# Two w_gate transfers of a GeGLU kernel on ScalarE's DMA queue: one issued three copies later, one taken over from SP's queue

## The chip, the cores and the metric

The kernel runs on one core of a Trainium2 chip. The metric is the device time of one execution in microseconds (us). Three runs of the kernel before took 275.5, 275.68 and 275.7 us; the median is 275.68 us.

## The reference

x is a bf16 tensor of 32 x 32 x 1024 values, seen as a 1024 x 1024 matrix (1024 tokens, D = 1024). w_gate and w_up are 1024 x 3584 (F = 3584), w_down is 3584 x 1024, all bf16.

```python
def reference(x, w_gate, w_up, w_down):
    return (_gelu(x @ w_gate) * (x @ w_up)) @ w_down     # _gelu: the tanh approximation
```

## The kernel before

Two stages follow each other: gate and up products with the Gelu between them (lines 131 to 353), then the product with w_down (lines 355 to 512). Each uses a scheme that needs seven block products in place of eight (sums of blocks are formed on VectorE, GpSimd and ScalarE first, then multiplied). The change touches only the start of the first stage.

The first stage works with transposed data: F is on the partitions, 28 blocks of 128 columns of F, and the tokens are the moving dimension, in two halves of 512. D is split in two halves of four 128-row pieces each (KH = 4). So there are four blocks of x: B11 and B21 (first 512 tokens, first and second half of D, together the tile xt0) and B12 and B22 (the other tokens, the tile xt1). The weights are a11 and a12 (the two halves of w_gate's rows for one block of F), a21 and a22 (those of w_up).

The order of the work is written out by hand (`tc.manual_schedule()`), and each engine and each DMA queue takes its own instructions in program order. What matters around the change:

- **Transposes of x**, all on SP's queue: L131 loads B11, L149 loads B21, L154 loads xt1. The one of L149 waits for a small ScalarE instruction (L147) that ends at 5.65 us.
- **w_gate** comes in tiles of two blocks of F, WG[c] for blocks 2c and 2c+1, each with a first half (`0, KH`, for a11) and a second half (`KH, DT`, for a12). `load_gate(c, queue, lo, hi)` (L83, the transfer in L86) loads a part of one: a half is 256 KB. WG[4] and WG[5] lie in parts of gT, the result of the stage, that are written much later; the others in a ring of four buffers.
- **ScalarE's queue** carries at the start (L140 to L145) the first halves of WG[0] to WG[3] and the second half of WG[0], and at L280 the second half of WG[1].
- **SP's queue** carries, behind the transpose of B21 (L149 to L157): the second half of WG[2], half of the first w_up tile WU[0], the second half of WG[3], all of WG[4], the transpose of xt1, the two halves of WG[5], the other half of WU[0]; later WG[6] (L319), which waits for a free buffer.
- **`first_products(n)`** (L204): four matmuls of block n, a11 by B11, then a ScalarE copy of the product (L212). **`second_products(n)`** (L214): four matmuls a12 by B21 onto the same PSUM bank, then a ScalarE Gelu (L219).
- PE's order is `first_products` of 0 and 1 together and of 2 to 7 one by one (L279 to L282), `second_products` of 0 to 7 (L283), `first_products` of 8 and 9, `second_products` of 8 and 9, `first_products(10)` (LEAD, L292), and then the products with sums of x: fifth (Y, with T1, L298), sixth (X, with T2), seventh (T3), fourth (T4). So block 2 is the first to use WG[1] in both parts, block 8 the first to use WG[4], block 10 the first to use WG[5].
- **The sums of x**: VectorE forms T1 to T4 (L166, called in L275 to L278) from xt1 and xt0; T1 in four pieces, the others in two each.

Of the kernel before, what the change touches and what calls it, by code (L numbers as in the profile page):

```python
# [12 lines left out]
def kernel(  # L13
# [18 lines left out]
    nc = tc.nc  # L32
# [10 lines left out]
    DT = D // P  # L43
    KH = DT // 2
# [38 lines left out]
    def load_gate(c, queue, lo=0, hi=DT):  # L83
        if c not in WG:
            WG[c] = gw.tile([P, DT, 2 * P], bf16, name="gw", tag="gw")
        queue.dma_start(  # L86
            out=WG[c][:, lo:hi, :], in_=wg_r[:, lo:hi, 2 * c * P : (2 * c + 2) * P]
        )
# [12 lines left out]
    def a11(i):  # L101
        return block(WG, 2, i, 0)

    def a12(i):
        return block(WG, 2, i, 1)
# [18 lines left out]
    def psum_p(name):  # L124
        return psum.tile([P, NB], fp32, name=name, tag="p")

    def psum_q(name):
        return psum.tile([P, NB], fp32, name=name, tag="q")

    with tc.manual_schedule():  # L130
# [21 lines left out]
        load_gate(3, nc.sync, KH, DT)  # L152
        load_gate(4, nc.sync)
        nc.sync.dma_start_transpose(out=xt1, in_=xf[NB:N, :])  # L154
        load_gate(5, nc.sync, 0, KH)
        load_gate(5, nc.sync, KH, DT)
        load_up(0, 2, 4)  # L157

# [32 lines left out]
        def pair_product(ps, lhs, rhs, first, cuts):  # L191
            for lo, hi in zip(cuts, cuts[1:]):
                for p, l in zip(ps, lhs):
                    for k in range(lo, hi):
                        nc.tensor.matmul(  # L195
                            p,
                            lhsT=l[:, k, :],
                            rhs=rhs[:, k, :],
                            start=(first and k == 0),
                            stop=(k == KH - 1),  # L200
                            skip_group_check=True,
                        )

        def first_products(*blocks, cuts=(0, KH)):  # L204
            for i in blocks:
                A[i] = psum_p("a") if 4 <= i < 8 else psum_q("a")
            pair_product([A[i] for i in blocks], [a11(i) for i in blocks], B11, True, cuts)
            for i in blocks:
                if i % 2 == 0:
                    pool, tag = (xpool, "e1") if i == LEAD - 2 else (ring, "ring")  # L210
                    E1[i // 2] = pool.tile([P, 2, NB], fp32, name="e1", tag=tag)
                nc.scalar.activation(E1[i // 2][:, i % 2, :], A[i], ACT.Copy)  # L212

        def second_products(*blocks, cuts=(0, KH)):  # L214
            pair_product([A[i] for i in blocks], [a12(i) for i in blocks], B21, False, cuts)
            for i in blocks:
                if i % 2 == 0:
                    GL[i // 2] = half.tile([P, 2, NB], bf16, name="gl0", tag="half")
                nc.scalar.activation(GL[i // 2][:, i % 2, :], A[i], ACT.Gelu_apprx_tanh)  # L219
# [3 lines left out]
        def seed(i):  # L223
            X[i] = psum_p("x")
            nc.scalar.activation(X[i], E1[i // 2][:, i % 2, :], ACT.Copy)
# [51 lines left out]
        t_sum("T3", B22, B12)  # L277
        t_sum("T4", B21, T["T2"])  # L278
        first_products(0, 1, cuts=(0, 2, KH))  # L279
        load_gate(1, nc.scalar, KH, DT)  # L280
        for n in range(2, 8):
            first_products(n)  # L282
        for n in range(8):  # L283
            second_products(n)
            if n in (5, 6):
                seed(n - 5)
        first_products(8)
# [255 lines left out]
```

## Time and profile before

| | |
|---|---|
| median of the runs | 275.68 us |
| the profiled execution | 275.76 us |
| its span, first to last instruction | 273.9 us |
| granted TensorE clock | 1.000 |
| PE (TensorE matmul) busy | 268.7 us, 98% of the span |
| VectorE, ScalarE, GpSimd busy | 69%, 51%, 32% |
| DMA in the whole span | 26.42 MB, mean 96 GB/s |
| DMA from 5.67 to 26.5 us | 269 to 311 GB/s |

How to read the lines that the prediction quotes: times are in us from the start of the span. A line of the timeline has the start, the duration, the engine, the source line, the operation, the tiles out<-in, shapes, the number of instructions merged in the line, and in brackets the idle time before it with what ended it. PE is TensorE's matmuls, PEld its weight loads, DVE is VectorE, ACT is ScalarE, POOL is GpSimd. SPq and ACTq are the DMA issues of SP and of ScalarE: their duration is that of the issue, not of the transfer; the time from issue to landing stands in another view. A line of the chain of waits has start, duration and what the chain ran through. A line of the table by stretches has the stretch, its length, the busy time and number of instructions of PE, PEld, DVE, ACT and POOL, the granted clock, the DMA share and GB/s.

### The profile page before, as it was taken

The numbers are of one execution on the slowest core, as the hardware profiler recorded it, in microseconds if no ns is written. First come the engines' busy times: TensorE is split into PE (matmuls) and PEld (weight loads), VectorE is DVE, ScalarE is ACT, GpSimd is POOL, SyncE is SP. The second block draws the span as 40 slices with busy tenths as digits, with TensorE's granted clock in tenths as the row PEclk, the third lists the DMA queues.
The fourth block names the chain that finished last, engine by engine and source line by source line (L and its number), as shares of the span: only waits on it lengthen the run. The fifth ranks groups of instructions, "written<-read, shape, count | busy, mean of one in ns | idle before, by whom it ended". The sixth has DMA issues, their size and how long they took to land.

```text
span 273.9 us, 3338 instructions
## 1 busy us (share of the span) xinstructions
PE 268.7 (98%) x1172; PEld 189.4 (69%) x1186; DVE 189.2 (69%) x226; ACT 139.7 (51%) x240; POOL 87.2 (32%) x81
## 2 busy tenths in 40 slices
PE   8999999999999999999999999999999999999995
PEld 2445677778777787776877768764447888888883
DVE  0078885866658666586665866769994999999900
ACT  4778665566565665666655666531100072860311
POOL 0000075745557455584555845600000000000000
PEclk9999999999999999999999999999999999999999
DMA  7999402153300034216360202369602000000321
GB/s 185 277 288 247 154 1 77 52 180 110 121 2 0 0 103 130 77 35 196 96 213 0 77 5 74 107 190 334 214 0 77 2 0 1 0 2 0 116 77 38
DMA packets 41024, 26.42 MB, mean 96 GB/s; under 512 B 9264, under 2 KB 41008, under 8 KB 41008
## 3 DMA queue, kind: packets, MB, share of 16 engines
q1 hardware_dynamic: 37680, 24.51, 30.5%
q10 hardware_dynamic: 3328, 1.70, 2.3%
q8 instruction: 9, 0.15, 0.2%
q14 instruction: 7, 0.06, 0.1%
HBM read 22.02 MB, written 2.10 MB: 88 GB/s over the span
## 4 chain that ended last, share of the span: by engine, by line
PE 94%; DMA 4%; ACT 1%; issue 0%
PE x L195 19%; PE x L398 18%; PE y L115 18%; PE a L195 15%; PE y L398 9%; PE x L115 9%; PE z L398 4%; DMA xt<-in_x_dram 3%; DMA gw<-in_w_gate_dram 1%; PE y L195 1%; ACT L139 0%; ACT o_sb L510 0%
## 5 line engine op out<-in xcount | busy, mean ns | idle before, releaser
L195 PE MATMUL x<-T,s 128*128 128x512 f32 x224 | 63.4, 407 | 0.0
L195 PEld LDWEIGHTS x<-T,s 128*128 128x128 f32 x224 | 41.7, 188 | 10.9 <-ACT e L242 0.3
L195 PE MATMUL a<-xt,gw 128*128 128x512 bf16 x182 | 44.1, 380 | 1.1 <-DMA xt<-in_x_dram 0.3
L259 DVE TENSOR_TENSOR u<-y,e 128x512 bf16<-128x512 f32 x28 | 19.3, 691 | 31.8 <-ACT e L257 30.9
L184 POOL TENSOR_TENSOR s<-gw,s 128x512 fp32r<-128x512 bf16 x22 | 26.0, 1182 | 47.6 <-PE y L115 46.9
L180 DVE TENSOR_TENSOR s<-s,gw 128x512 fp32r<-128x512 f32 x24 | 34.9, 1456 | 0.0
L195 PEld LDWEIGHTS <-gw 128*128 128x128 bf16 x192 | 17.1, 98 | 24.8 <-issue 5.2
L266 ACT ACTIVATE gl<-h 128x512 bf16<-128x512 bf16 x28 | 17.7, 631 | 27.5 <-DVE h L264 27.5
L246 DVE TENSOR_TENSOR gT<-gl,x 128x512 bf16<-128x512 bf16 x28 | 19.2, 686 | 17.9 <-PE x L115 17.9
L115 PE MATMUL x<-T,c 128*128 128x512 f32 x112 | 30.3, 392 | 0.0
L115 PE MATMUL y<-B,s 128*128 128x512 f32 x112 | 30.2, 391 | 0.0
L175 POOL TENSOR_TENSOR s<-uw 128x512 fp32r<-128x512 bf16 x25 | 29.1, 1165 | 0.0
L115 PE MATMUL y<-T,s 128*128 128x512 f32 x104 | 27.8, 389 | 0.0
L398 PE MATMUL x<-tc,sc 128*128 128x512 f32 x112 | 25.7, 389 | 0.0
L257 ACT ACTIVATE e<-x 128x512 f32<-128x512 f32 x28 | 16.7, 600 | 16.0 <-PE x L195 16.0
L176 POOL TENSOR_TENSOR s<-gw,uw 128x512 fp32r<-128x512 bf16 x21 | 24.5, 1167 | 0.0
L115 PEld LDWEIGHTS y<-B,s 128*128 128x128 f32 x112 | 21.0, 188 | 4.8
L212 ACT ACTIVATE e<-a 128x512 f32<-128x512 f32 x28 | 16.6, 597 | 15.2 <-PE a L195 15.2
L115 PEld LDWEIGHTS x<-T,c 128*128 128x128 f32 x112 | 20.9, 188 | 4.8 <-ACT e L257 0.4
L398 PEld LDWEIGHTS x<-tc,sc 128*128 128x128 f32 x112 | 21.0, 188 | 4.4
L115 PEld LDWEIGHTS y<-T,s 128*128 128x128 f32 x104 | 19.5, 188 | 4.1
L219 ACT ACTIVATE gl<-a 128x512 bf16<-128x512 f32 x28 | 16.7, 597 | 7.1 <-PE a L195 7.0
(58 smaller groups left out, 342.0 us busy)
## 6 DMA issues: line engine op xcount, KB each, us to landing
uw<-in_w_up_dram SPq DMA_DIRECT2D x6, 1024.0 KB, 6.4
gw<-in_w_gate_dram SPq DMA_DIRECT2D x8, 512.0 KB, 4.0
v<-in_w_down_dram SPq DMA_DIRECT2D x5, 512.0 KB, 3.8
v<-in_w_down_dram SPq DMA_DIRECT2D x4, 640.0 KB, 8.1
v<-in_w_down_dram SPq DMA_DIRECT2D x8, 256.0 KB, 4.2
out_dram<-o_sb SPq DMA_DIRECT2D x15, 128.0 KB, 1.7
gw<-in_w_gate_dram ACTq DMA_DIRECT2D x5, 256.0 KB, 5.0
uw<-in_w_up_dram SPq DMA_DIRECT2D x2, 512.0 KB, 5.4
```

Source lines behind the costliest of these rows:

```text
L115: nc.tensor.matmul(ps, lhsT=lhs[:, k, :], rhs=rhs[:, k, :], start=(first and k == 0), stop=(k == KH - 1), skip_group_check=True,)
L175: engine.tensor_tensor(S1[i], a21(i), a22(i), ALU.add)
L176: engine.tensor_tensor(S3[i], a11(i), a21(i), ALU.subtract)
L180: nc.vector.tensor_tensor(S2[i], S1[i], a11(i), ALU.subtract)
L184: engine.tensor_tensor(S4[i], a12(i), S2[i], ALU.subtract)
L195: nc.tensor.matmul(p, lhsT=l[:, k, :], rhs=rhs[:, k, :], start=(first and k == 0), stop=(k == KH - 1), skip_group_check=True,)
L219: nc.scalar.activation(GL[i // 2][:, i % 2, :], A[i], ACT.Gelu_apprx_tanh)
L246: nc.vector.tensor_tensor(gT[:, i, 0:NB], GL[i // 2][:, i % 2, :], X[i], ALU.mult)
L257: nc.scalar.activation(e3, X[i], ACT.Copy)
L259: nc.vector.tensor_tensor(U1[i], Y[i], e3, ALU.add)
L266: nc.scalar.activation(G1[i], h1, ACT.Gelu_apprx_tanh)
L398: nc.tensor.matmul(ps, lhsT=lhs[:, i, t * P : (t + 1) * P], rhs=rhs[:, i, :], start=(first and j == 0 and i == 0), stop=(last and j == JF ...
```

## The change

The second half of WG[1] is still loaded over ScalarE's queue, but its issue stands behind the copy of `first_products(3)` (the fourth copy) and no longer behind the first two. The first half of WG[5] is no longer issued by SP, behind the transpose of xt1, but by ScalarE, behind the Gelu of `second_products(1)` (the second Gelu). Its second half stays on SP's queue. No instruction is added or removed.

```diff
         nc.sync.dma_start_transpose(out=xt1, in_=xf[NB:N, :])
-        load_gate(5, nc.sync, 0, KH)
         load_gate(5, nc.sync, KH, DT)
         load_up(0, 2, 4)
...
         first_products(0, 1, cuts=(0, 2, KH))
-        load_gate(1, nc.scalar, KH, DT)
         for n in range(2, 8):
             first_products(n)
+            if n == 3:
+                load_gate(1, nc.scalar, KH, DT)
         for n in range(8):
             second_products(n)
+            if n == 1:
+                load_gate(5, nc.scalar, 0, KH)
             if n in (5, 6):
                 seed(n - 5)
```

## The prediction

> **What bounds the kernel now.** I read the page first. Its first part says that TensorE is what the span consists of, and the chain of work that ended last says the same (PE 94%, DMA 4%):
>
> ```profile
> PE 268.7 (98%) x1172; PEld 189.4 (69%) x1186; DVE 189.2 (69%) x226; ACT 139.7 (51%) x240; POOL 87.2 (32%) x81
> ```
>
> So the change can win only where the chain is not PE. I then took the chain in order of time over the first 36 us. It leaves PE in two places: the first weights (until 5.41) and one transpose of x:
>
> ```profile
> 5.41 0.26 PE a L195
> 5.67 7.18 DMA xt<-in_x_dram
> 12.86 0.14 issue
> 12.99 1.67 PE a L195 x7
> ```
>
> The transpose is that of L149 (B21): issued at 5.67, landed at 12.86, and `second_products(0)` starts at 12.99. What the wait costs is not the 0.28 us that the waits list shows for it (matmuls overlap). I read it from ScalarE, which copies one product each time PE has done four matmuls:
>
> ```profile
> 10.16 0.60 ACT L212 ACTIVATE e<-a 128x512 f32<-128x512 f32 x1 [0.27 <-PE a L195]
> 11.02 0.60 ACT L212 ACTIVATE e<-a 128x512 f32<-128x512 f32 x1 [0.27 <-PE a L195]
> 11.89 0.60 ACT L212 ACTIVATE e<-a 128x512 f32<-128x512 f32 x1 [0.27 <-PE a L195]
> 12.75 0.60 ACT L212 ACTIVATE e<-a 128x512 f32<-128x512 f32 x1 [0.27 <-PE a L195]
> 14.05 0.60 ACT L219 ACTIVATE gl<-a 128x512 bf16<-128x512 f32 x1 [0.70 <-PE a L195]
> ```
>
> The step is 0.863 us (0.216 per matmul). After the copy at 12.75 the next event is due at 13.61 and comes at 14.05: PE lost **0.44 us**, and from 13 us on PE has no further stall before 24 us. 0.44 us is 0.16% of the time. Less than 0.2% (0.55 us) is about what a measurement of this kernel cannot tell from no change.
>
> Last, why does the transpose land so late? The timelines of SP's queue and of ScalarE's:
>
> ```profile
> 5.67 3.97 SPq L149 DMA_TRANSPOSE xt<-in_x_dram  x1
> 7.54 0.37 ACTq L86 DMA_DIRECT2D gw<-in_w_gate_dram  x1
> 9.70 0.58 SPq L86 DMA_DIRECT2D gw<-in_w_gate_dram  x1
> 12.46 6.84 SPq L154 DMA_TRANSPOSE xt<-in_x_dram  x1
> 19.34 1.13 SPq L86 DMA_DIRECT2D gT<-in_w_gate_dram  x2
> 21.52 2.50 DVE L166 TENSOR_TENSOR T<-xt,xt 128x512 fp32r<-128x512 bf16 x4 [1.04 <-DMA xt<-in_x_dram]
> ```
>
> The ACTq row at 7.54 is the second half of WG[1] (I call it the gate-1 tail), issued in the middle of the transpose's issue. The first row at 19.34 holds two issues: WG[5]'s first half (the gate-5 head) and its second. The trace also holds a record of each DMA packet. There the transpose's data packets run from 8.6, when ScalarE's earlier transfers run out, to 11.05. Then the gate-1 tail's 256 KB run on the same engines from 11.0 to 11.85, and only at 11.77 to 11.86 come the transpose's 32 four-byte packets, which end it. For the two other transposes these packets come with the last data (data to 4.35, packets at 4.20 to 4.39; data to 20.9, packets at 20.91 to 20.95). So the gate-1 tail stands between the transpose's data and its landing for 0.7 us. The moved rate has a hole before that, too:
>
> ```profile
> 8.00:9.00 1.00, 1.00 (x6) 0.49 (x5) 0.00 (x0) 0.75 (x2) 0.00 (x0) 1.00 1.21 284
> 9.00:10.00 1.00, 1.00 (x7) 0.43 (x5) 0.00 (x0) 0.63 (x2) 0.00 (x0) 1.00 1.34 168
> 10.00:11.00 1.00, 1.00 (x6) 0.45 (x5) 0.00 (x0) 0.60 (x1) 0.00 (x0) 1.00 1.27 289
> ```
>
> The last column is GB/s: in 9 to 10 some 120 KB were not moved, about 0.42 us at 289. Whether the 7.54 issue made that hole the trace does not show.
>
> **Part 1, the gate-1 tail behind the fourth copy.** ScalarE issues a DMA when it has sent off the copy before it, not when the copy ends: the 7.54 issue stands between the first copy's start (7.10) and the second's (7.60). So the new issue comes with the fourth copy, at 9.30: 1.76 us later. Cost on ScalarE: 0.37 us (the row above) against 0.26 us idle per step; the next copy is 0.11 us late, and the step after has it back. The first user of a freed PSUM bank, `first_products(8)`, comes at 19.89, 5 us behind the first Gelu's end. So this costs nothing; without that cover it would be 0.37.
>
> Gain: if the transpose ends with its data, its end packets come at 11.1 in place of 11.8, and it lands at about 12.15 or earlier (12.86 - 0.7). PE's next weight load is due at 12.34 (last at 12.12, step 0.216), and it began 0.10 behind the landing: a landing by 12.24 loses nothing. So the whole 0.44 returns. The bounds: 0 (the order of the packets stays), and 0.44, for then PE's own work ends last, whatever else the queue gains.
>
> What is late next: the gate-1 tail itself. `second_products(2)` loads its weights at 14.50 now, at 14.06 with PE 0.44 earlier. On an idle queue the first packet came 1.04 us after the issue (28.64, 40.80); so its data can run from 11.05, 256 KB at 289 GB/s take 0.91, and it lands between 12.5 and 13.0. Cover 1 us. SP's next, the second half of WG[2], shares that stretch, lands at 13.50 now, and is needed at 16.2: cover 2.7 us, 2.2 after the shift.
>
> **Part 2, the gate-5 head on ScalarE's queue.** SP's row at 19.34 loses one issue (0.58 us), so the WG[5] tail and the last half of WU[0] follow at once, 0.6 earlier; WG[6] waits at 21.08 for its buffer, as now. ScalarE issues at the second Gelu, 14.91 now, 14.47 shifted: 0.37 to 0.57 us (five issues in 2.83 at the start) beside 0.26 idle per Gelu, so up to 0.3 us late, made good in two Gelus, and nobody waits until 19.89.
>
> What it removes is a limit that part 1 would run into. The gate-5 head lands now at 19.34 + 3.7 = 23.04, and `first_products(10)` loads its first weights at 23.14: 0.10 us of cover. With PE 0.44 earlier alone, 0.34 would be lost there. Issued at 14.5 it is there by 22.4 even if it is served only behind the whole third transpose (data to 20.9, then 0.91, then 0.6 to land). Cover 0.3 of the shifted need at 22.70.
>
> What it adds: 256 KB ahead of the landing of the third transpose (12.46 + 9.0 = 21.46), on which DVE's T1 waits (1.04 us idle). At 289 GB/s that is **0.91 us**. The bounds: 0 (served later), and 1.7, if it meets all that the second transpose meets now (0.91 of data, the hole's 0.42, and some 0.3 of increments behind the other's). I take 0.91: the transfer has the size of the gate-1 tail, whose packets took 0.85. Cover: T1's fourth piece ends at 24.02 and the matmul that reads it starts at 25.60; T2's second half ends at 26.29, its reader starts at 27.86. Both leave 1.57, less 0.07 from DVE to PE: 1.50, and 1.06 with PE shifted. 0.91 fits, by 0.15. T3, T4 have 2.0.
>
> **Sum**: -0.44 (part 1) + 0 (ScalarE) + 0 (part 2 uses up cover only) = -0.44. The profiled execution took 275.76 us (span 273.9 and 1.86 around it): 275.32. The median of the runs is 275.68, 0.08 lower: 275.24. I say **275.3**.
>
> **The rivals.**
>
> *The landing stays (A).* The new issue at 9.30 still falls before SP has finished issuing the transpose (9.64). If what counts is that ScalarE's transfer comes into the queue before the transpose's end packets do, the order stays, B21 lands at 12.86, and part 2 has its 1.5 us of cover: 275.7. For it: with 1.04 from issue to data the tail is ready at 10.34, before the data end at 11.05. Against: so was the first transfer of ScalarE (issue 1.83) while the first transpose ran until 4.35, and that one's end packets were not held up. The Trainium skill (DMA: Bandwidth & Descriptors, section "Queues, rings and completion order") says that the increment of a semaphore lands only after every earlier write of that DMA engine, across its queues. By that rule B21 lands late as long as the tail's data is taken first, which is this rival; the end packets at 11.77 agree with it.
>
> *ScalarE's queue is left waiting (B), the slower side.* The second transpose was issued at 5.67 and had no packet until 8.6, exactly as ScalarE's backlog ran dry. If a queue with work keeps the engines, the reverse holds: the gate-1 tail, now issued only 0.4 us ahead of SP's 9.70, waits behind WG[2]'s half and WU[0] and lands where that lands now, at 15.33, against a need at 14.06. From a landing after 14.0 it costs PE time: 15.4 + 0.1 - 14.06 = 1.4, less the 0.44: 276.7 and more if the gate-5 head, needed at 22.70, meets the same. Against: at 11.0 the tail got in although SP's transfer of 9.70 should have been ready at 10.74. The same section of the Trainium skill says that an engine goes round the queues that have work, packet by packet; by that rule this rival falls. The trace shows no such mixing around 8.6, so I keep the rival.
>
> *The third transpose is later than 0.91 (C).* At 1.2 to 1.7, T1 and T2 exceed their 1.06 by 0.15 to 0.65: 275.4 to 275.9.
>
> *A stall that I do not see goes too (D)*: below 275.1.
>
> **How the numbers follow.** Forecast 0.52, A 0.17, B 0.13, C 0.12, D 0.06. Faster by over 0.2% (below 275.13) takes D and 0.06 of the forecast, which ends 0.1 to 0.2 us from that line: 0.12. Slower by over 0.2% (above 276.23) takes B and 0.03 of C: 0.16. Within: 0.72. The range runs from 275.0 to 276.7: it takes in A, C and B's price for the gate-1 tail alone, and leaves out B's worse end and most of D.
>
> **What would show it.** Right: no chain piece of the L149 transpose behind PE's last `first_products` matmul; its landing by 12.3; the first Gelu at 13.6; the first product on gT at 19.45; T1 beginning by 22.5 with PE unbroken from 24 to 28. Part 1 wrong: the first Gelu still at 14.05 (A), or a PE wait on gw near 14.1 (B). Part 2 wrong: a PE wait on gT near 22.7, or on DVE T between 23.6 and 28 (C).

## The result, and the profile after

The changed kernel takes 276.0 us (median of 22 runs, 275.55 to 276.88) against 275.68 us for the kernel before (22 runs beside them, 275.02 to 276.2). The ratio is 1.0013, with a 95% interval of 1.0008 to 1.0019: slower by a little more than a tenth of a per cent, where 275.3 us, 0.14% faster, had been forecast. All ratios here leave out an execution more than 1.5% above the fastest of its kernel; there was one such, of 279.78 us, in after_third below. The profiled execution of the changed kernel took 275.71 us (span 273.9). That is near the low end of its runs; a profile of a longer one comes below.

I read the new profile in the order of the old one. The busy times of the page are the same within 0.1 us on every engine: nothing has changed in the amount of work. Then ScalarE's timeline of the changed kernel around the first Gelu, with start, duration, engine, line and idle time (the lines of the kernel file have moved up by one behind the edit):

```profile
12.69 0.60 ACT L211 ACTIVATE e<-a 128x512 f32<-128x512 f32 x1 [0.27 <-PE a L194]
13.55 0.60 ACT L218 ACTIVATE gl<-a 128x512 bf16<-128x512 f32 x1 [0.27 <-PE a L194]
14.42 0.40 ACTq L86 DMA_DIRECT2D gT<-in_w_gate_dram  x1
```

The step of 0.863 us now runs on from the last copy (12.69) to the first Gelu (13.55). The 0.44 us that PE lost there are gone. The last copy was 0.06 us earlier already (12.69 against 12.75), so the first Gelu is 0.50 us earlier than before (14.05). Part 1 did what it was to do. The transpose of L149 lands at 11.23 in place of 12.86.

So PE was half a microsecond ahead and ended where it had ended before. The chain of waits of the changed kernel, in order of time, tells where it was given back (start, duration, what the chain ran through):

```profile
12.74 9.80 DMA xt<-in_x_dram
...
22.63 3.65 DVE T L165 x5
...
26.31 5.63 DVE T L165 x5
31.94 0.16 DVE u L258
...
34.34 0.60 DVE s L179
34.95 0.60 DVE gT L245
35.54 0.61 DVE h L263
36.16 0.02 issue
36.18 0.64 ACT gl L265
...
38.11 0.59 ACT e L241
38.69 0.04 issue
38.74 2.14 PE x L194 x8
```

In the kernel before, every piece of this stretch was PE. Now it begins with the third transpose (xt1, landed at 22.54; before at 21.43), goes through ten VectorE instructions for T1 to T4, and then, and this is what the reader is to see, it does not go from a T sum to its PE reader. It goes on along VectorE's own queue: u (L258), the sums of block 2, h (L263), a Gelu and a copy on ScalarE, and only there back to PE, at 38.74. (Some short pieces are left out.) VectorE's timelines of the two kernels show the same place. Before:

```profile
31.88 1.29 DVE L259 TENSOR_TENSOR u<-y,e 128x512 bf16<-128x512 f32 x2 [1.05 <-ACT e L257]
```

After:

```profile
22.63 2.50 DVE L165 TENSOR_TENSOR T<-xt,xt 128x512 fp32r<-128x512 bf16 x4 [1.84 <-DMA xt<-in_x_dram]
...
29.59 2.35 DVE L165 TENSOR_TENSOR T<-xt,T 128x1024 fp32r<-128x1024 bf16 x2
31.86 1.28 DVE L258 TENSOR_TENSOR u<-y,e 128x512 bf16<-128x512 f32 x2
```

Before, VectorE had 1.05 us free between T4 and the first u, and waited there for ScalarE, which waited for PE; T4 had ended at 30.83. After, the bracket is gone: the first u follows T4 at once. It starts at 31.86, 0.02 us from where it started before, and so does all that follows.

PE's rows tell how the lead of 0.50 us went. Before, the last four matmuls ahead of the fourth products, and the weight load of the seventh products of block 2:

```profile
31.52 1.04 PE L195 MATMUL a<-xt,gT 128*128 128x512 bf16 x4
38.76 1.69 PEld L195 LDWEIGHTS x<-T,s 128*128 128x128 f32 x8 [0.34 <-ACT e L242]
```

After:

```profile
31.22 1.04 PE L194 MATMUL a<-xt,gT 128*128 128x512 bf16 x4
38.73 1.70 PEld L194 LDWEIGHTS x<-T,s 128*128 128x128 f32 x8 [0.61 <-ACT e L241]
```

At 31 us PE is still 0.30 us ahead: 0.20 us went between 24 and 28 us, where weight loads waited for T1 and T2. At 38.7 us 0.03 us are left: 0.27 us went into the longer wait, 0.61 us in place of 0.34, for the copy at the end of the chain from u.

### The profile page after: what moved, and what is told of

Same layout as the page of the kernel before. It is cut to its first block, busy times and chain, and to the rows that moved or that the text cites. A ratio compares the mean times of both kernels' runs of the same rounds, so it can differ in the third digit from the quotient of the medians.

```text
span 273.9 us, 3340 instructions
## 1 busy us (share of the span) xinstructions
PE 268.8 (98%) x1172; PEld 189.4 (69%) x1186; DVE 189.1 (69%) x226; ACT 139.6 (51%) x240; POOL 87.1 (32%) x81
## 4 chain that ended last, share of the span: by engine, by line
PE 86%; DVE 5%; DMA 5%; ACT 1%; SPq 1%; issue 1%; DVEq 0%
PE x L400 18%; PE x L194 17%; PE y L115 17%; PE a L194 11%; PE y L400 9%; PE x L115 9%; PE z L400 4%; DMA xt<-in_x_dram 4%; DVE T L165 3%; DMA gw<-in_w_gate_dram 1%; SPq L86 1%; DVE h L263 0%; ACT L139 0%; DVE u L258 0%; ACT gl L265 0%
## 5 line engine op out<-in xcount | busy, mean ns | idle before, releaser
L194 PEld LDWEIGHTS x<-T,s 128*128 128x128 f32 x224 | 41.6, 188 | 11.3 <-ACT e L241 0.6
L258 DVE TENSOR_TENSOR u<-y,e 128x512 bf16<-128x512 f32 x28 | 19.3, 691 | 30.8 <-ACT e L256 30.0
```

The lines of the kernel that those rows point to most:

```text
L194: nc.tensor.matmul(p, lhsT=l[:, k, :], rhs=rhs[:, k, :], start=(first and k == 0), stop=(k == KH - 1), skip_group_check=True,)
L258: nc.vector.tensor_tensor(U1[i], Y[i], e3, ALU.add)
```

## The experiments

Two theories went in. **V**: the change loses what it gains, and more, because the third transpose lands later and VectorE's queue, T1 to u and on, carries that to PE. **G**: the gate-1 tail (the second half of WG[1]), now issued later, is what is late in many runs. Later expectations name two more. **W**: what the change costs lies in transfers that are late for PE itself, or in ScalarE's issues. **H**: the gate-5 head (the first half of WG[5]) is what comes late for PE when SP's queue carries it. Ratios are to the kernel before, run beside each kernel on the same chip. All numbers of a profile are of one execution.

One number served in all of them: how far the last matmul's start lies behind the start of the first u.

| kernel | third transpose lands | T4 ends | first u | last matmul | distance |
|---|---|---|---|---|---|
| before | 21.43 | 30.83 | 31.88 | 270.32 | 238.44 |
| changed | 22.54 | 31.94 | 31.86 | 270.30 | 238.44 |
| part1_only | 21.94 | 31.35 | 31.77 | 270.27 | 238.50 |
| part2_only | 22.32 | 31.73 | 31.95 | 270.42 | 238.47 |
| head_after_sixth_gelu | 23.24 | 32.65 | 32.56 | 271.04 | 238.48 |
| head_doubled | 23.92 | 33.32 | 33.24 | 271.69 | 238.45 |
| head_before_transpose | 22.42 | 31.82 | 31.74 | 270.20 | 238.46 |
| after_again | 22.27 | 31.68 | 31.59 | 269.94 | 238.35 |
| after_third | 22.21 | 31.62 | 31.53 | 270.00 | 238.47 |
| after_look_a | 22.99 | 32.40 | 32.31 | 270.77 | 238.46 |
| after_look_b | 22.05 | 31.45 | 31.37 | 269.84 | 238.47 |
| split_in_after | 20.72, 22.48 | 30.12 | 31.38 | 269.88 | 238.50 |
| split_in_before | 19.70, 21.62 | 29.20 | 31.59 | 270.08 | 238.49 |
| split_part1 | 20.51, 22.50 | 30.10 | 32.41 | 270.79 | 238.38 |
| split_part2 | 20.57, 22.00 | 29.98 | 31.65 | 269.98 | 238.33 |
| split_before_again | 19.87, 21.80 | 29.45 | 31.81 | 270.25 | 238.44 |
| split_tail_on_SP | 21.85, 23.90 | 31.26 | 31.61 | 270.09 | 238.48 |

Whatever was changed in the first 24 us, the distance stays within 238.33 to 238.50. So the effect lies ahead of the first u, and the time is that start plus a constant, within 0.2 us. (Two landings are those of a transpose issued in two.) The first u starts at the later of two things: T4's end (it then stands 0.08 or 0.09 us ahead of it, since VectorE's instructions overlap a little), or PE's seventh products and ScalarE's copy of them.

**The two parts alone.** part1_only is the kernel before with this edit:

```diff
-        load_gate(1, nc.scalar, KH, DT)
         for n in range(2, 8):
             first_products(n)
+            if n == 3:
+                load_gate(1, nc.scalar, KH, DT)
```

> Only the gate-1 tail is moved; the gate-5 head stays on SP's queue. Theory V (the loss comes from the third transpose landing late, through VectorE's queue, which runs without a gap from T1 to the work behind T4): the first Gelu starts near 13.55 as after the change, the third transpose lands at 21.5 or earlier, VectorE has idle time again before L259 (0.3 us or more), and the time is 0.1 to 0.45 us under the kernel before: 275.25 to 275.6. If the gate-5 head lands at 23.0, PE waits up to 0.35 us for it near 22.7, which takes most of that. Rival G (the gate-1 tail, issued later, is what is late in many runs and stalls second_products(2)): 276.0, as with the whole change.

Measured: 275.74 us, ratio 1.0002 (0.9993 to 1.0012). That is over the range of V, and no gain. The interval just reaches G's 276.0, but the trace speaks against G: no weight load of PE waits for a transfer into gw (the ring that takes the tail) after 8 us, here or in any other profile. What took the lead is the gate-5 head: still on SP's queue, it lands at 23.19, and PE waits for it. The third transpose, though nothing was put ahead of it, lands at 21.94, half a microsecond later than before and later than V expected; in this execution that took only some of VectorE's rest. From the list of waits of part1_only between 13 and 32 us (engine, line, what it waited for: us, times, longest):

```profile
DVE T L166 <- DMA xt<-in_x_dram: 1.1, 1, 1.1
PEld L195 <- DMA gT<-in_w_gate_dram: 0.5, 1, 0.5
DVE u L259 <- ACT e L257: 0.4, 1, 0.4
```

The last line is VectorE's rest before u: 0.4 us of 1.05 are left, so here u waits for PE and not for T4.

part2_only is the kernel before with the other edit:

```diff
-        load_gate(5, nc.sync, 0, KH)
...
             second_products(n)
+            if n == 1:
+                load_gate(5, nc.scalar, 0, KH)
```

> Only the gate-5 head goes over ScalarE's queue, behind the second Gelu; the gate-1 tail stays where it was. Theory V: the first Gelu stays at 14.05, the third transpose lands 0.9 to 1.2 us later than before (22.3 to 22.6), VectorE begins L259 with no idle time, and the time is 0 to 0.5 us over the kernel before: 275.7 to 276.2, about that of the whole change. Rival G: the gate-1 tail is not touched, so the time stays within 0.1 us of before.

Measured: 275.77 us, ratio 0.9997 (0.9985 to 1.0009). The third transpose lands at 22.32, 0.89 us later than before, as V says; the rest of VectorE before u shrinks to 0.2 us and is not used up, where V had expected none left, since PE is not ahead here. The time fits V, and G too; the next runs tell more.

**The cost doubled, and the head moved.** head_doubled adds a second transfer of 256 KB, which nobody needs, to the changed kernel:

```diff
             if n == 1:
                 load_gate(5, nc.scalar, 0, KH)
+                extra = gT[:, FT - 6 : FT - 4, :].rearrange("p a (b f) -> p (a b) f", f=2 * P)
+                nc.scalar.dma_start(out=extra[:, 0:KH, :], in_=wg_r[:, 0:KH, 0 : 2 * P])
```

> The whole change, and behind the gate-5 head a second transfer of 256 KB over ScalarE's queue into a part of gT that is written later and that nobody reads before: the suspected cost doubled. Theory V: the third transpose lands 0.9 us later than after the change (23.4 to 23.6), VectorE's work from T1 on moves by as much, and the time rises by 0.8 to 0.9 us to 276.7 to 277.0. Rival G, or slack left behind VectorE: 276.0 to 276.2.

Measured: 277.16 us (5 runs), ratio 1.0051 (1.0039 to 1.0064). The third transpose lands at 23.92, 1.38 us behind the changed kernel's 22.54; the first u starts 1.38 us later (33.24 against 31.86) and the profiled time is 1.45 us longer (277.16 against 275.71). The size was over what I expected, because 256 KB cost this transpose more than the 0.9 us of their data; but microsecond for microsecond it goes through to the end. This is V's clearest run. The chain of head_doubled:

```profile
12.38 11.54 DMA xt<-in_x_dram
...
24.01 3.64 DVE T L165 x5
...
27.69 5.63 DVE T L165 x5
33.32 0.17 DVE u L258
```

head_after_sixth_gelu issues the gate-5 head later (`if n == 5` in place of `if n == 1`):

> Both parts, but the gate-5 head is issued behind the sixth Gelu (about 17.9) in place of the second. Theory V: its data come behind most or all of the third transpose, which lands near 21.5, VectorE has its idle time before L259 back, and the time falls under the kernel before: 275.3 to 275.6, unless the gate-5 head now lands after 22.7, which costs PE what it is late. Rival G: 276.0, as the whole change, for the gate-1 tail is the same.

Measured: 276.21 us, ratio 1.0019 (1.001 to 1.0028). The expectation failed, and the packets show how. The head's data did come behind the transpose's: the transpose's data run to 21.54 and the head's from 21.41 to 22.30. But the transpose did not land at 21.5: it landed at 23.24, behind the head. That is what the prediction had read of the second transpose and the gate-1 tail, now at the third: a transfer of the other queue, standing between a transpose's data and its end packets. VectorE's u follows T4 at once here too (32.56), so V holds; only the cure was none. The head itself landed at 22.97, late enough for PE to wait 0.3 us for it.

head_before_transpose, the last version that was run, goes the other way, with the head issued behind the seventh copy, ahead of SP's issue of the transpose:

```diff
             if n == 3:
                 load_gate(1, nc.scalar, KH, DT)
+            if n == 6:
+                load_gate(5, nc.scalar, 0, KH)
...
-            if n == 1:
-                load_gate(5, nc.scalar, 0, KH)
```

> Both parts, but the gate-5 head is issued behind the seventh copy, near 11.8, before SP issues the third transpose, so that its data are moved ahead of that transpose and not among or behind them. Theory V: the third transpose lands 0.9 to 1.1 us later than before (22.3 to 22.5), the first u stands at the end of T4, and the time is 275.4 to 275.8. If the spread of the changed kernel (medians of 275.59, 276.0 and 276.37) comes from where the head falls among the transpose's data, the runs here lie within 0.6 us. Rival: the spread stays, 1 us or more, and has another cause.

Measured: 275.85 us, ratio 1.001 (1.0001 to 1.0018), runs from 275.52 to 276.16. The transpose lands at 22.42, within what V said, and the first u stands at T4's end. The median is a little over the range. The 12 runs spread by 0.64 us, against 1.33 for the changed kernel in its 22 runs, but the kernel before, run beside them, spread by 0.93 in 17. So whether the head's place makes the spread stays open. The head's data (15.1 to 17.0 in the packets) were all moved ahead of the transpose's, and it landed a microsecond later all the same.

**VectorE's wait taken away.** If V is right, the change must pay once VectorE no longer waits for the whole third transpose. T1 needs only its first half, B12. So the transpose is issued as two, same bytes, same queue:

```diff
-        nc.sync.dma_start_transpose(out=xt1, in_=xf[NB:N, :])
+        nc.sync.dma_start_transpose(out=B12, in_=xf[NB:N, 0 : KH * P])
+        nc.sync.dma_start_transpose(out=B22, in_=xf[NB:N, KH * P : D])
```

> The whole change, and the third transpose issued as two, B12 first and then B22: the same bytes, but T1, which needs B12 alone, can begin before B22 has landed. This takes away VectorE's wait and moves T1 to T4 ahead by about 1.5 us. Theory V: VectorE has idle time before the first u again, PE keeps what part 1 gave (first Gelu near 13.55), and the time is 275.2 to 275.4, under both kernels. Rival W (what the change costs lies in the transfers that are late for PE itself, or in ScalarE's issues): 275.9 to 276.1, as the change.

Measured: 275.21 us, ratio 0.9986 (0.9977 to 0.9995), runs from 275.0 to 275.52. This is the version that beats both kernels (the changed one, run beside it, took 275.59), and its time is the one forecast for the change. B12 lands at 20.72, B22 at 22.48, as late as in the changed kernel; but T1 has begun at 20.82. VectorE's timeline of split_in_after:

```profile
20.82 2.50 DVE L166 TENSOR_TENSOR T<-xt,xt 128x512 fp32r<-128x512 bf16 x4
...
31.38 1.29 DVE L259 TENSOR_TENSOR u<-y,e 128x512 bf16<-128x512 f32 x2 [1.26 <-ACT e L257]
```

The bracket is back: VectorE waits for PE, not PE for VectorE. The first u is at 31.38, 0.50 us ahead of the kernel before, which is the whole lead of the first Gelu. The changed kernel's transfers, its ScalarE issues and its late gate-1 tail are all still there, so W falls. The split ends both waits on T sums at once, that of u and those of PE's weight loads for T1 and T2; of the two, u was the larger by PE's rows above (0.27 against 0.20 us), and the one that ended last.

The control is the same split in the kernel before:

> The kernel before with the third transpose in two, and nothing else. Theory V: PE sets the first u there, not VectorE, and the second transpose still lands near 12.85, so earlier T sums bring nothing: 275.6 to 275.8. If the split by itself made the kernel faster by 0.3 us or more, the gain of the split in the changed kernel would not speak for theory V.

Measured: 275.86 us, ratio 1.0015 (1.0006 to 1.0025), runs from 275.43 to 276.69. It is no gain, as V says, but over the range: the split alone makes the kernel slower. Nor did the second transpose land near 12.85: it landed at 12.35, and PE lost nothing behind it (last copy 12.88, first Gelu 13.74). So PE was 0.31 us ahead, and waited 0.34 us for the gate-5 head, which lands at 23.00 on SP's queue, behind both halves of the transpose. Theory H was made for this. The two parts were tried by themselves with the split in place.

> The third transpose in two, and the gate-1 tail behind the fourth copy; the gate-5 head stays on SP's queue. Theory H (with VectorE's wait gone, the gate-5 head on SP's queue is what comes late: it lands at 23.0, and PE, ahead by 0.3 to 0.5 us, needs it at 22.6 to 22.8): PE waits on gT near 22.7, and the time is 275.5 to 276.0, over that of the split with both parts (275.2). Rival: the gate-5 head matters only through VectorE, and the time is that of the split with both parts, 275.2 to 275.3.

Measured: 276.27 us, ratio 1.0022 (1.0014 to 1.0031). The head lands at 20.52 + 3.3 = 23.82. PE's timeline of split_part1:

```profile
22.30 1.03 PE L196 MATMUL a<-xt,gT 128*128 128x512 bf16 x4
23.87 1.04 PE L196 MATMUL a<-xt,gT 128*128 128x512 bf16 x4 [0.54 <-DMA gT<-in_w_gate_dram]
```

Four matmuls begin at 22.30; the next should follow in 0.86 and follow in 1.57: 0.7 us lost to the head. That is more than I expected for this kernel, and its first u (32.41) is late by as much, with VectorE idle (T4 ended at 30.10).

> The third transpose in two, and the gate-5 head over ScalarE's queue; the gate-1 tail stays behind the second copy. Theory H: the second transpose lands at 12.3 to 12.9 as in the kernel before, so PE starts late, nothing else is late any more, and the time is 275.5 to 275.7, with less spread than the split in the kernel before. Rival: the spread of that kernel (275.4 to 276.7) has another cause than the gate-5 head, and stays.

Measured: 275.58 us, ratio 1.0002 (0.9993 to 1.0011), runs from 275.37 to 275.94. The second transpose lands at 12.61, PE comes late behind it (last copy 12.51, first Gelu 13.81) and waits for no transfer from there to 32 us, and the runs spread by 0.57 us in place of the 1.26 of split_in_before. So H is borne out on both sides: on SP's queue the head is late for PE, and with part 2 that wait and the longer times are gone.

> The split in the kernel before once more, to see a profile of one of its slower executions if one comes. Theory H: where the time is over 275.8, PE has a wait on gT near 23, of the size of the excess. Rival: PE has no such wait, and the excess lies elsewhere before 32 us.

Measured: 275.93 us (8 runs, ratio 1.0019, 1.001 to 1.0029); the profiled execution took 275.73. In the list of waits of that kernel, 13 to 32 us:

```profile
DVE u L260 <- ACT e L258: 2.4, 1, 2.4
PEld L196 <- DMA gT<-in_w_gate_dram: 0.5, 1, 0.5
```

There is the wait for the head, while VectorE rests for 2.4 us. The profiled one was not over 275.8, so what the executions of 276.3 and more lose has not been seen; that it is the head is argued from split_part2.

split_tail_on_SP sends the gate-1 tail over SP's queue behind the second transpose, with the split and part 2:

```diff
         nc.sync.dma_start_transpose(out=B21, in_=xf[0:NB, KH * P : D])
+        load_gate(1, nc.sync, KH, DT)
         load_gate(2, nc.sync, KH, DT)
...
-            if n == 3:
-                load_gate(1, nc.scalar, KH, DT)
```

> As the split in the changed kernel, but the gate-1 tail goes over SP's queue, directly behind the second transpose, so that no transfer of ScalarE's can come between that transpose's data and its end packets. Theory V: the second transpose lands at 11.2 to 12.0 in every run, the first Gelu comes at 13.5 to 13.6, and the time is that of the split in the changed kernel or up to 0.2 us less: 275.1 to 275.4. Rival W: 275.9 to 276.1.

Measured: 275.45 us, ratio 0.9993 (0.9984 to 1.0002). That is a little over the range. The second transpose lands at 11.44. The first Gelu is at 13.78, later than expected: PE's first matmul came late in that execution, at 5.80 (5.46 in the changed kernel), and ScalarE's steps from the fourth copy to the Gelu are all of 0.86 or 0.87 us. The halves of the third transpose land at 21.85 and 23.90, more than a microsecond later than in split_in_after. It is no better than split_in_after.

**The changed kernel again.** after_again and after_third are the changed kernel with nothing edited.

> The changed kernel once more, for a second profile. Theory V: its time goes with the start of VectorE's L259 instruction (the first u), which follows the third transpose's landing: in five profiles so far the last matmul starts 238.4 to 238.5 us behind that start. So again the last matmul at the first u plus 238.45, and a time over 275.7 by what the third transpose lands later than 22.5. Rival: the end moves against the first u by more than 0.2 us, and the cause lies behind it.

Measured: 275.59 us, ratio 1.0006 (0.9997 to 1.0014); the profiled execution 275.35.

> The changed kernel a third time, for one more profile. Theory V: last matmul 238.4 to 238.5 us behind the first u, and the first u directly at the end of T4, with no idle time of VectorE between T1 and it.

Measured: 276.37 us, ratio 1.0029 (1.0015 to 1.0043), eight runs from 275.42 to 279.78; the profiled execution 275.42. The distance to the first u is as expected in both (the first 0.05 us short), and the first u stands at T4's end. The medians differ between batches by 0.8 us, so the loss is not one fixed number. Two more executions were profiled, to see a long one.

> The changed kernel, one look, for a profile of a slower execution if it comes. Theory V: whatever the time, the last matmul is 238.4 to 238.5 us behind the first u, and the first u follows the landing of the third transpose by 9.2 to 9.4 us. Rival: a slow execution loses its time elsewhere.

> As the look before it: the last matmul 238.4 to 238.5 us behind the first u, and the first u 9.2 to 9.4 us behind the third transpose's landing, also in a slower execution.

Measured: 276.19 and 275.26 us. The third transpose landed at 22.99 and 22.05, the first u came at 32.31 and 31.37: 9.32 us behind the landing in both, as in the three other profiles of this kernel (9.32 each). The two times differ by 0.93 us, the two landings by 0.94. So the long execution lost its time to the third transpose too. VectorE's timeline of after_look_a:

```profile
23.09 2.50 DVE L165 TENSOR_TENSOR T<-xt,xt 128x512 fp32r<-128x512 bf16 x4 [1.88 <-DMA xt<-in_x_dram]
...
32.31 1.29 DVE L258 TENSOR_TENSOR u<-y,e 128x512 bf16<-128x512 f32 x2
```

Why it landed later there is seen only in part. The table by stretches (its last column is GB/s) has a hole in the transfers as the transpose's data begin:

```profile
17.00:18.00 1.00, 1.00 (x6) 0.47 (x5) 0.97 (x3) 0.60 (x1) 0.00 (x0) 1.00 1.87 206
18.00:19.00 1.00, 1.00 (x7) 0.47 (x5) 1.00 (x2) 0.96 (x2) 0.00 (x0) 1.00 0.82 202
```

The changed kernel's first profile moved 239 and 294 GB/s there. That is some 125 KB more, about 0.43 us at 290 GB/s, which is nearly all of the 0.45 us between the two landings (22.54, 22.99).

## Why the prediction was wrong, step by step

*What bounds the kernel, and the 0.44 us.* Right for the execution that it was read from. The stall behind the second transpose was 0.44 us there, the tail stood between that transpose's data and its end packets, and with part 1 the stall was gone. But 0.44 us is what one execution lost. Four more profiles have the tail in its old place. In split_part2 the stall is there again, of 0.44 us. In part2_only, split_in_before and split_before_again the first Gelu follows the last copy by 0.86 us (13.24 to 14.11, 12.88 to 13.74, 12.92 to 13.79): PE came 0.1 to 0.5 us later there, the transpose landed a little earlier (12.81, 12.35, 12.60), and nothing was lost. So the full 0.44 us was not to be had in the median.

*ScalarE's cost: nothing.* Right. The new issues begin at 9.24 and 14.42, with the copy at 9.23 and the Gelu at 14.41, and the steps of 0.863 us run on.

*The gate-1 tail lands between 12.5 and 13.0, in time.* Right: 9.24 + 3.7, about 12.9, and no PE wait near 14.

*The gate-5 head would be the next limit without part 2.* Right, and shown twice: a weight load waits 0.5 us for it in part1_only, and PE loses 0.7 us in split_part1. That it lands by 22.4 with part 2 was right with room: 14.42 + 6.2, about 20.6.

*The third transpose lands 0.91 us later.* Near: 1.11 us in the first profile, 0.62 to 1.56 over five. I had put it down to part 2 alone. In part1_only, where only the tail was moved, it landed 0.51 us later than before, so the late tail seems to cost it something as well; that is one profile, and the landings of the changed kernel alone differ by 0.94 us. There, and in the changed kernel, the transfers have a hole among the tail's first packets: in the changed kernel the stretches 10 to 11 and 11 to 12 moved 230 and 165 GB/s, where they had moved 289 and 340 before.

*Cover for it: T1 to T4 against the matmuls that read them, 1.06 us with PE shifted.* **This is the step that failed.** I counted the slack of each T sum to its reader on PE and stopped there; the sum's "0 (part 2 uses up cover only)" rests on it. I did not ask what stands behind T4 on VectorE itself. That is u, with 1.05 us of rest before it in the kernel before; and the chain from u over h, a Gelu and a copy to the seventh products of block 2 was already level with PE: in the kernel before, too, the weight load of those products, at 38.76, had waited 0.34 us for that copy. When PE moves ahead by 0.5 us, u is wanted earlier by as much, and of 1.05 us about 0.55 are left: too little for 0.91, let alone 1.11. By that reckoning the gain could not be 0.44 us; the first u moves by the transpose's delay less 1.05 us, but no further ahead than PE's lead. For 1.11 that is 0.06 us later; it was 0.02 us earlier, since u starts 0.08 us ahead of T4's end.

*The sum of -0.44 us*, then, was a lead at 24 us and not at the end. Rival C had the right transfer and looked for its harm at T1 and T2's readers. There was some: by the waits list weight loads waited 0.5 us for T1 and 0.2 for T2, and 0.20 us of PE's lead went there. But even without it the lead would have ended at u.

*Rival A* (the landing stays) did not happen in the profile. It is not dead: in head_after_sixth_gelu, head_doubled and after_look_a the second transpose landed at 12.55, 12.12 and 12.53, with its end packets behind or among the tail's, and in after_look_a PE lost 0.3 us by it. Its rule from the Trainium skill (DMA: Bandwidth & Descriptors, section "Queues, rings and completion order"), that an increment lands only after the engine's earlier writes of all queues, agrees with these.

*Rival B* (ScalarE's queue is left waiting) did not come about: the tail landed in time, and the head, whose first packet came 4.2 us after its issue, landed 2 us ahead of its need. From 18.8 to 19.8 the packets of the two queues alternate, 80 to 88 of each in every 0.2 us. That is the round by packets of the same section of the Trainium skill, which I had kept at a distance because nothing around 8.6 showed it. In the kernel before, at 8.6 and 11.0, the queues took turns in long blocks, and the runs don't show when it is the one and when the other.

What stays open: why the transfers have holes (at 9.1 to 9.7 before, 10.8 to 11.3 after, 17.6 to 18.3 in after_look_a), and so why the third transpose's landing varies by a microsecond between executions. That the longer executions of the changed kernel lose their time to it is shown in one profile, after_look_a (the other four are of executions of 275.71 us or less), and supported by split_in_after, which has the same transfers, no wait of VectorE for them, and runs within 0.52 us.

## What to carry to other kernels

A late input is not covered by the slack of its readers alone; the engine that works on it must have slack too, up to the first instruction in its queue that waits for someone else. Look for the bracket with the idle time on that engine's timeline: it is the real cover, and if it is PE that ends it, it shrinks by whatever PE gains. And where a transfer is moved out of the way of one transfer, see which comes next on the same engines; here the next one fed VectorE, whose work PE waited for later.

## What the runs showed of the hardware

A plain transfer issued on one queue while a DMA transpose is being issued on the other can hold the transpose's end: data complete at 21.54, landing at 23.24, with the 256 KB of the other transfer between them (head_after_sixth_gelu). It is not so each time: the second transpose landed at 11.10 to 11.41 in eight profiles with the tail issued behind the fourth copy, at 8.92 to 9.56, and at 12.12 to 12.55 in three others with the tail issued in the same stretch.

A transfer issued on ScalarE's queue in the middle of a transpose's issue on SP's took 4.2 us to its first packet (14.42 to 18.61), against 1.04 us on an idle queue. The transpose's issue need not be the reason: SP's earlier transfers ran until 17.6, and in head_before_transpose a transfer issued ahead of the transpose's issue, at 11.83, took 3.3 us.

One transpose of 1 MB issued as two of 512 KB lands its first half 1.8 us ahead of the second (20.72, 22.48), and the second no later than the whole one in the same kernel (22.54), in one profile of each.
